# The first chunk's triangular inverses: squarings on TensorE against a 16x16 solve on VectorE, in a two-stage kernel on one Trainium2 core

## The chip, the cores and the metric

The kernel runs on one core of one Trainium2 chip. Its time is the device time of one execution in microseconds (us), of which smaller is better. The span is the part of an execution that the profiler's records cover.

## The reference

Two stages follow each other. The first is a recurrence over 768 steps for each of 4 x 8 heads, with a state of 40 x 40:

```python
for t in range(S):                      # S = 768; r, k, v, w, a, b are (4, 8, 768, 40), float32
    y[:, :, t] = np.einsum('bhd,bhde->bhe', rt, state)
    Sa = np.einsum('bhde,bhe->bhd', state, at)
    state_decay = state * wt[:, :, None, :] - np.einsum('bhd,bhe->bhde', Sa, bt)
    state = state_decay + np.einsum('bhd,bhe->bhde', vt, kt)
```

Its output, as x of 3072 x 320 (heads side by side), goes through a feed-forward block with an exact GELU:

```python
h = x @ w_in                            # w_in is 320 x 2048, passed as 64-bit floats
g = 0.5 * h * (1.0 + erf(h * inv_sqrt2))
out = (g @ w_out).astype(np.float32)    # w_out is 2048 x 320, passed as 64-bit floats
```

## The kernel before

**Chunks.** The 768 steps are cut into 12 chunks of C = 64. Within a chunk the recurrence is written as products: masked 64 x 64 matrices between the columns of a, b, k, r and v, which are scaled by running products of w. Each of the 32 heads needs the inverse of one unit triangular 64 x 64 matrix, whose strict part is N. Two blocks of 32 x 32 on its diagonal are inverted, and a product of three joins them. NBL = 16 heads lie side by side in the free dimension, and two batches one above the other in the 128 partitions.

**Steps.** Every piece of work is a small function marked `@step`; a suffix names the chunk. For chunk c the steps that matter here are these.

- `lg`, `cu`, `ec`, `wT`, `ew`: logarithm of w, running sums by matmuls (L717, L708), their exponentials.
- `sb`, `sk`: b and k scaled by these decays (L796, L801). `sk.0` runs on GpSimd before, `sk.1` and `sk.2` on VectorE.
- `ta`, `tb`, `tk`, `tr`, `tv`: turned on TensorE in chunks 0 to 2 (L763), copied out by `sa`, `sn`, `kc`, `rc`, `vc`.
- `nm`, `am`, `vm`: the 64 x 64 products (L188); `nk`, `ak`, `vk` mask them on VectorE (L876).
- `nd`, `nx`, `iz`, `ic`, `wx`: for chunks 1 to 11 the 32 x 32 inverses by column elimination on GpSimd (L957, L959, 62 operations for a chunk). `nx` brings N into the tile `Nb`, `iz` sets the tile `W` to the identity, `wx` takes the result to `Tt`.
- `tc_`, `jm`, `jc`, `wb`, `km`, `kt0`, `kt1`, `wa`: the joining product.
- `av`, `xm`, `xc0`, `xc1`, `sm`, `sc`, `pk`, `pb`, `oa`, `od`, `om`: the chunk's result and the next state. For chunk 0 `xp` and `xe` (L1244) bring the result into `xt`, for others `ox` by DMAs.
- `mh` (eight per chunk, L1308), `ge`: x @ w_in and the GELU; chunk 0 then has four `pm` (L1429), and the others seven products `m1` to `m7` (L1347, with sums `s1` to `s4`, `e1` to `e6` on VectorE and ScalarE) for g @ w_out.
- `Lf`, `Lf5`, `Ls`: the weights as 64-bit words, in 18 units; `ce`, `cs`, `cm`, `cv` (or `cl`, `cn`, `cg`, `cx`, `cy`) turn each unit into 32-bit floats. Units 0 to 9 are w_in. Unit 9 lies in the memory of `xt` until `cv.9` has read it, so `xe` comes behind `cv.9`.
- `warm_first`, `warm`: matmuls whose results nobody reads.

**Chunk 0.** Its 32 x 32 inverses are made otherwise: as a product of (I + N^(2^k)). `qt`, `qi`, `qs` start it; `qm.0` to `qm.4` multiply on TensorE, `qz` turns on VectorE, `qb` and `qs` split into two halves on VectorE and ScalarE, `qc` copies on ScalarE, `qa` adds on VectorE; `ql` and `qx` place the result, and `jm.0`, `jc.0`, `km.0` join with forms of their own.

**Order.** One text, `order`, names every step once, and the program is issued in just this order. Each engine works through its own instructions in it, and waits only where data or a buffer asks for it. PSUM is held as four tiles `bank0` to `bank3`, taken in turn by `take` and given back by `drop`; all DMAs of the stretch discussed here are issued from SyncE, in the order's sequence.

Of the kernel before, what the change touches and what calls it, by code (L numbers as in the profile page):

```python
# [1467 lines left out]
```

## Time and profile before

| | |
|---|---|
| median of 3 runs | 632.1 us (631.37 to 632.44) |
| profiled execution | 632.67 us, span 630.9 us |
| mean granted TensorE clock | 0.995 |
| busy: TensorE matmuls, weight loads | 619.7 us (98%), 521.8 us (83%) |
| busy: VectorE, ScalarE, GpSimd | 454.4 (72%), 345.4 (55%), 369.6 us (59%) |
| DMA | 63.97 MB, mean 101 GB/s |

In the profile PE is TensorE's matmuls, PEld its weight loads, DVE VectorE, ACT ScalarE, POOL GpSimd, SP SyncE. A line number is that of the kernel before; L188 is the helper `mm`, so matmuls of many steps carry it and are told apart by their tiles. Matmuls overlap, so the time from the first start to the last end of a group says more than its mean. A matmul of 32-bit floats in the source is two instructions in the trace. The granted clock is in shares of full speed. The profiled execution lies 1.8 us over its own span and 0.6 us over the median.

### The profile page before, as it was taken

To read this page: it belongs to the slowest core of one execution; us is meant where nothing else is said; L and a number is where in the kernel's file an instruction comes from. 1 tells how busy PE (TensorE), PEld (TensorE's weight loads), DVE (VectorE), ACT (ScalarE), POOL (GpSimd) and SP (SyncE) were. 2 spreads that over 40 slices of the span, in tenths; PEclk is the share of its full clock that TensorE was granted. 3 is DMA by queue.
4 is the path that set the end of the run, shared out by engine and by line. 5 is a ranking of instruction groups with operands and counts; after the bars stand their busy time and mean duration, and the time that the engine had idled before them with its cause. 6 is when DMAs were issued, how large, how long until landed. Compare 5 with 4: busy or idle time off the path is not lost.

```text
span 630.9 us, 31485 instructions
## 1 busy us (share of the span) xinstructions
PE 619.7 (98%) x14196; PEld 521.8 (83%) x14196; DVE 454.4 (72%) x558; ACT 345.4 (55%) x475; POOL 369.6 (59%) x797
## 2 busy tenths in 40 slices
PE   8989999999999999999999999999999999999997
PEld 5777787777987987987987988987988978978977
DVE  1788998875979978996886785875867955744313
ACT  4866897685454637636654647445557435243020
POOL 6278565738814875868848818838813886830000
PEclk9998999999999999999999999999999999999999
DMA  9997887722555766665575554444663454110100
GB/s 153 166 155 166 188 181 175 132 62 47 117 109 86 146 116 119 128 124 102 98 133 101 108 108 87 83 77 96 123 132 51 85 87 86 34 25 4 43 3 21
DMA packets 246550, 63.97 MB, mean 101 GB/s; under 512 B 228216, under 2 KB 243328, under 8 KB 246416
## 3 DMA queue, kind: packets, MB, share of 16 engines
q1 hardware_dynamic: 245976, 61.68, 52.0%
q8 instruction: 111, 1.82, 1.2%
q10 hardware_dynamic: 440, 0.29, 0.2%
q14 instruction: 23, 0.19, 0.1%
HBM read 54.39 MB, written 3.93 MB: 92 GB/s over the span
## 4 chain that ended last, share of the span: by engine, by line
PE 95%; ACT 1%; DVE 1%; SPq 1%; issue 1%; DMA 0%; DVEq 0%; ACTq 0%
PE bank L1308 33%; PE bank L188 30%; PE bank L1347 27%; PE bank L1429 3%; PE bank L763 2%; SPq L479 0%; SPq L1226 0%; DMA xt<-xt 0%; ACT st L1016 0%; DVE os L1298 0%; ACT L727 0%; ACT N L918 0%; DVE N L876 0%; ACT kT L727 0%; ACT gt L1313 0%
## 5 line engine op out<-in xcount | busy, mean ns | idle before, releaser
L1308 PE MATMUL bank<-xt,w_in_sb 64*64 64x256 f32 x3840 | 220.5, 377 | 1.1 <-DMA xt<-xt 1.1
L957 POOL TENSOR_TENSOR tmp<-W,Nb 128x126 f32<-128x126 f32 (+22 forms) x341 | 156.9, 460 | 77.3 <-DVE Nb L923 51.7
L1308 PEld LDWEIGHTS bank<-xt,w_in_sb 64*64 64x64 f32 x3840 | 147.1, 133 | 52.1 <-issue 1.8
L959 POOL TENSOR_TENSOR W<-W,tmp 128x126 f32<-128x126 f32 (+22 forms) x341 | 163.7, 480 | 26.7
L1347 PE MATMUL bank<-w_out_sb,gt 128*128 128x160 f32 x704 | 102.0, 302 | 0.2 <-ACT gt L1313 0.2
L1347 PEld LDWEIGHTS bank<-w_out_sb,gt 128*128 128x128 f32 x704 | 96.6, 190 | 3.5 <-issue 1.3
L1313 ACT ACTIVATE gt<-bank 128x1024 f32<-128x1024 f32 x48 | 49.1, 1024 | 73.1 <-PE bank L1308 71.9
L1152 DVE TENSOR_TENSOR SM<-bank,upper 128x832 f32<-128x832 f32 (+1 forms) x24 | 22.9, 989 | 19.5 <-PE bank L188 19.4
L1262 ACT COPY conv<-st 32x128 f32<-32x128 f32 (+2 forms) x55 | 28.0, 510 | 14.5 <-DVE st L1256 13.7
L1298 DVE TENSOR_TENSOR os<-os,bank 128x160 f32<-128x160 f32 x44 | 14.0, 319 | 28.5 <-PE bank L1347 19.1
L1347 PE MATMUL bank<-extra,conv 128*128 128x160 f32 x208 | 30.0, 299 | 0.0
L1313 ACT ACT_TABLE_LOAD x23 | 29.5, 1283 | 0.4
L1298 DVE TENSOR_TENSOR conv<-gt 128x1024 f32<-128x1024 f32 x11 | 14.0, 1272 | 21.0 <-ACT gt L1313 21.0
L1347 PEld LDWEIGHTS bank<-extra,conv 128*128 128x128 f32 x208 | 28.9, 190 | 0.0
L1204 DVE TENSOR_TENSOR st<-bank,st 128x832 f32<-128x832 f32 (+1 forms) x22 | 21.2, 986 | 8.8 <-PE bank L188 8.8
L1347 PE MATMUL bank<-extra,gt 128*128 128x160 f32 x176 | 26.4, 303 | 0.2 <-DVE os L1298 0.2
L734 DVE TENSOR_TENSOR_SCAN kT<-spare,kT 128x256 f32<-128x256 f32 x36 | 26.1, 782 | 0.6 <-ACT kT L727 0.6
L1347 PEld LDWEIGHTS bank<-extra,gt 128*128 128x128 f32 x176 | 24.3, 190 | 1.5 <-issue 0.9
L942 POOL MEMSET W<- 128x512 f32 x11 | 5.8, 525 | 32.9 <-DVE Tt L928 32.9
L801 POOL TENSOR_TENSOR bk_rows<-bk_rows,part 128x640 f32<-128x640 f32 x9 | 14.5, 1614 | 14.1 <-DMA bk_rows<-in_k_dram 14.1
L699 ACT ACT_TABLE_LOAD x11 | 14.1, 1283 | 13.8 <-DMA w_tile<-in_w_dram 13.7
L754 ACT ACT_TABLE_LOAD x11 | 14.1, 1283 | 13.1 <-PE bank L188 12.7
(227 smaller groups left out, 1156.1 us busy)
## 6 DMA issues: line engine op xcount, KB each, us to landing
bk_rows<-in_b_dram SPq DMA_DIRECT2D x24, 160.0 KB
bk_rows<-in_k_dram SPq DMA_DIRECT2D x24, 160.0 KB
out_dram<-os SPq DMA_DIRECT2D x46, 80.0 KB
VR<-in_v_dram SPq DMA_DIRECT2D x22, 160.0 KB
w_tile<-in_w_dram SPq DMA_DIRECT2D x36, 80.0 KB
v_pairs<-in_w_dram SPq DMA_DIRECT2D x18, 144.0 KB
a_pairs<-in_a_dram SPq DMA_DIRECT2D x18, 144.0 KB
a_pairs<-in_b_dram SPq DMA_DIRECT2D x18, 144.0 KB
```

Of the source, the lines that this page charges most:

```text
L188: nc.tensor.matmul(o, lhsT, rhs, start=first, stop=True, skip_group_check=True)
L734: nc.vector.tensor_tensor_scan(logs[:, at:at + n], onward, logs[:, at:at + n], 0.0, ALU.mult, ALU.add)
L957: nc.gpsimd.tensor_tensor(t, W[:, BL // 2 - rows:, rest:rest + 1].to_broadcast([P, rows, rest]), Nb[:, rest:rest + 1, :rest].to_broadcast( ...
L959: nc.gpsimd.tensor_tensor(own, own, t, ALU.add)
L1152: nc.vector.tensor_tensor(SM[:, g, :, :, cols], pair_of(f"S{c}_", g).rearrange("p x i c -> p i x c")[:, :, :, cols], kept, ALU.mult)
L1204: nc.vector.tensor_tensor(to, pair_of(f"QY{c}_", g)[:, :, :, cols], to, ALU.add)
L1262: nc.scalar.copy(apart.rearrange("p e i g d -> p (e i g) d")[to_rows, :, to_col:to_col + n], st.rearrange("p e i g c -> p (e i g) c")[rows ...
L1298: nc.vector.tensor_tensor(to, one_, other, how)
L1308: nc.tensor.matmul(ph[half(x ^ y), x, s], w_in_sb[half(x), kt, at:at + HP], xt[half(x), kt], start=kt == 0, stop=kt == NK - 1, skip_group_ ...
L1313: nc.scalar.activation(gt[:, 4 * q:4 * q + 4].rearrange("p (x s) t -> p x s t", x=2), bank(f"ph{c}_{q}").rearrange("p x (s t) -> p x s t", ...
L1347: nc.tensor.matmul(po[:, n, :DM // 2], l_[:, f], r_[:, f], start=f == 0, stop=f == NF // 2 - 1)
L1429: nc.tensor.matmul(po[:, g, :DM], gt[:, f, g * P:(g + 1) * P], w_out_sb[:, f], start=f == 0, stop=f == NF - 1)
```

## The change

Chunk 0's 32 x 32 blocks are no longer inverted by squarings. Each is cut into two blocks of 16 x 16; `dx` and `dh` bring all of them into `N_16`, `dz` sets `W_16` to the identity, and `de` solves them by column elimination on VectorE, 15 columns of two operations each. `dw` and `dt` bring the result to `Tt`, `tc_.0` turns it; `dm`, `dj`, `dk.0`, `dl`, `dk.1`, `da` join the 16 x 16 blocks to 32 x 32 in both orientations by products on TensorE: 64 products of 32 x 32 by 32 x 16 in `dm`, 32 in `dk.0`, 64 in `dk.1`. From there chunk 0 uses `jm`, `jc`, `wb`, `km`, `wa` as the other chunks do. `sk.0` runs on VectorE. The tile `of_half` and the steps `diagonal_set` and `of_half_set` go, `parity` gets a third row. `N_16`, `W_16` and the turned blocks lie in the tile `Nb`, and `dj` writes into the tile `W`. The order text is another one throughout, for all twelve chunks; `one_set` stands late in it. The branches of `iz`, `ic` and `L_of` for chunks from 12 on, which no chunk took, are gone.

```diff
-        eng.tensor_tensor(T_, stacked, diagonal.unsqueeze(1).to_broadcast([P, NBL, BL]), ALU.add)
-    def qm(k):
-        take(f"sq{k}", (2, 3, 3, 3, 1)[k])
...
+    QL = BL // 2
+    turned_16 = Nb_tile[:, :QL * BL]
+    N_16 = Nb_tile[:, QL * BL:QL * BL + QL * QL].rearrange("p (t s) -> p t s", s=QL)
+    W_16 = Nb_tile[:, QL * BL + QL * QL:].rearrange("p (t s) -> p t s", s=QL)
+    J_16 = W_tile.rearrange("p (n t) -> p n t", t=BL)
+    T_of_0 = flat(Tt)[:, :, BL:]
...
+    def dx():
+        nc.vector.transpose(turned_16.rearrange("p (t n z) -> p t n z", n=NBL, z=2),
+                            halves(flat(N_of(0))[:, :, :BL]))
+    def dh():
+        both = turned_16.rearrange("p (t z s) -> p t z s", z=2, s=QL)
+        nc.vector.scalar_tensor_tensor(N_16, both[:, :, 0], parity[:, 0, 0:1], both[:, :, 1], ALU.mult, ALU.add)
+    def de(j0, j1, q):
+        for u in range(QL - 1 - j0, QL - 1 - j1, -1):
+            n = QL - u
+            t = tmp_tile[:, :n * u].rearrange("p (s t) -> p s t", s=n)
+            own = W_16[:, u:, :u]
+            eng.tensor_tensor(t, W_16[:, u:, u:u + 1].to_broadcast([P, n, u]),
+                              N_16[:, u:u + 1, :u].to_broadcast([P, n, u]), ALU.mult)
+            eng.tensor_tensor(own, own, t, ALU.add)
+    def dw(z, q):
+        to, keep = turned_16.rearrange("p (t z s) -> p t z s", z=2, s=QL)[:, :, z], parity[:, z, 0:1]
+        if q == "a":
+            nc.scalar.mul(to, W_16, keep)
+        else:
+            nc.vector.tensor_scalar(to, W_16, keep, None, ALU.mult)
+    def dt():
+        nc.vector.transpose(halves(T_of_0), turned_16.rearrange("p (t n z) -> p t n z", n=NBL, z=2))
+    def dm():
+                mm(J[rows, n, :QL], N[rows, n, own], L_tile[rows, n, :QL])
+    def dj():
+        nc.scalar.mul(J_16[:, :, :QL], J[:, :, :QL], parity[:, 2, 0:1])
+    def dk(z):
+                if z:
+                    mm(K[rows, n, :QL], J_16[rows, n], T_of_0[rows, n, QL:])
+                elif q % 2 == 0:
+                    mm(K[rows, n, :QL], T_of_0[rows, n], J_16[rows, n, :QL])
+    def dl(x):
+        nc.vector.tensor_tensor(own, K[lo[x], :, :QL], own, ALU.add)
+    def da():
+        nc.vector.tensor_tensor(own, K[:, :, :QL], own, ALU.add)
```

The order up to the first `mh`, where TensorE's steps stand in this sequence. Before:

```
warm_first warm.4.4 cu.0 wT.0 ta.0 tb.0 warm.4.2 nm.0 cu.1 warm.4.15 wT.1 qm.0 warm.4.20 tb.1 ta.1 qm.1 nm.1 cx.1 tk.0
qm.2 warm.4.0 am.0 qm.3 tr.0 tv.0 qm.4 vm.0 jm.0 warm.4.13 av.0 km.0 cu.2 sm.0 warm.4.18 pk.0 pb.0 tv.1 wT.2 tb.2 ta.2
xp.0 tk.1 nm.2 xp.1 tr.1 am.1 tk.2 warm.4.24 vm.1 mh.0.0
```

After:

```
warm.4.13 warm.4.20 warm.4.25 cu.0 wT.0 tb.0 ta.0 nm.0 cu.1 wT.1 tv.0 warm.4.18 warm.4.4 warm.4.15 warm_first ta.1 dm
tb.1 tr.0 dk.0 dk.1 warm.4.24 nm.1 tk.0 cx.1 jm.0 vm.0 am.0 cu.2 km.0 av.0 tv.1 sm.0 tk.1 ta.2 pk.0 pb.0 wT.2 xp.0 xp.1
tr.1 tb.2 vm.1 nm.2 warm.4.0 am.1 mh.0.2
```

VectorE's steps of the new order from `nk.0` to `xe.1`:

```
nk.0 dx dh de.0.5 de.5.10 de.10.15 dw.1 dt tc_.0 sb.1 cs.0 cs.1 cm.0 cv.0 cm.1 sa.1 dl.0 da dl.1 sk.0 cs.2 cm.2 nk.1 cv.2
nx.1 cy.1 vk.0 ak.0 sk.1 cs.3 cm.3 cv.3 xc1.0 kt1.0 cs.4 cm.4 cv.4 sc.0.0 sc.0.1 cs.5 cm.5 cv.5 od.0.0 om.0.0 om.0.1 cs.6
cm.6 od.0.1 cs.7 cm.7 cv.7 sb.2 sa.2 cs.9 cm.9 cv.9 vk.1 xe.1
```

More of the change, by code (lines that the diff above doesn't have):

```diff
@@ L363, in diagonal_set @@
     @step
-    def diagonal_set():
-        for q in range(P // BL):
-            rows = slice(q * BL, (q + 1) * BL)
-            nc.gpsimd.tensor_copy(diagonal[rows], ident[rows, rows])
-    @step
     def sums_mask():
@@ new lines, in dw @@
+    @step
+    def dw(z, q):
[4 more added lines that the diff above has]
+            nc.vector.tensor_scalar(to, W_16, keep, None, ALU.mult)
+    @step
+    def dt():
+        nc.vector.transpose(halves(T_of_0), turned_16.rearrange("p (t n z) -> p t n z", n=NBL, z=2))
+    @step
+    def dm():
+        N = flat(N_of(0))
+        J = take("D0")[:, 0].rearrange("p (n t) -> p n t", n=NBL)
+        for n in range(NBL):
+            for q, rows in enumerate(quads):
+                own = slice(q % 2 * BL, (q % 2 + 1) * BL)
+                mm(J[rows, n, :QL], N[rows, n, own], L_tile[rows, n, :QL])
@@ L1434, in pc @@
         drop(f"po{c}")
-    for token in order(NCH, NS):
+    for token in order():
         perform(steps, token)
```

329 lines of the change are left out of this document (132 added, 197 removed).

## The prediction

> **What bounds the kernel.** I read the page first: busy times and the chain that ended last.
>
> ```profile
> PE 619.7 (98%) x14196; PEld 521.8 (83%) x14196; DVE 454.4 (72%) x558; ACT 345.4 (55%) x475; POOL 369.6 (59%) x797
> ...
> PE 95%; ACT 1%; DVE 1%; SPq 1%; issue 1%; DMA 0%; DVEq 0%; ACTq 0%
> ```
>
> TensorE is nearly always busy and makes 95% of the chain. But a share over the whole span hides that the start is of another kind. So I cut the span by windows, at the start of the squarings (17.9), of chunk 0's `sm` (55.3), of the first `mh` (78.9) and of the first `pm` (101.3). The columns after the length are PE, PEld, DVE, ACT, POOL, granted clock, DMA share, GB/s.
>
> ```profile
> 0.00:17.90 17.90, 15.22 (x132) 9.10 (x132) 3.82 (x6) 9.31 (x11) 10.29 (x57) 1.00 0.97 159
> 17.90:55.30 37.40, 34.27 (x818) 27.52 (x817) 30.07 (x48) 28.55 (x41) 22.98 (x50) 0.91 0.93 153
> 55.30:78.90 23.60, 23.56 (x510) 19.09 (x512) 22.20 (x38) 18.40 (x25) 14.92 (x33) 1.00 0.84 190
> 78.90:101.30 22.40, 22.40 (x644) 18.35 (x632) 19.96 (x30) 20.85 (x31) 9.92 (x20) 1.00 0.83 176
> 101.30:631.00 529.70, 524.23 (x12119) 447.75 (x12112) 378.35 (x439) 268.27 (x372) 311.45 (x638) 1.00 0.47 89
> ```
>
> From 78.9 on TensorE is idle for 5.5 of 552.1 us. So the end moves with the start of the first `mh`, plus whatever work lies behind it. Before that, TensorE's busy share includes fillers (`warm`), squarings and slow matmuls, and VectorE is close behind. The start is therefore the place where this change is won or lost. In finer windows, one dip shows in it:
>
> ```profile
> 42.00:44.00 2.00, 1.96 (x80) 1.71 (x76) 1.93 (x5) 1.82 (x4) 1.76 (x4) 1.00 1.46 170
> 44.00:46.00 2.00, 0.08 (x5) 0.08 (x7) 1.90 (x3) 0.64 (x1) 1.76 (x4) 0.71 0.66 73
> 46.00:48.00 2.00, 2.00 (x66) 1.88 (x68) 0.66 (x2) 1.86 (x2) 1.69 (x5) 0.50 0.93 160
> 48.00:50.00 2.00, 2.00 (x28) 1.04 (x24) 1.97 (x4) 1.32 (x4) 1.76 (x4) 0.50 0.66 93
> ```
>
> After a gap of 1.9 us at 44 the granted clock is 0.50 until 50, so "busy" there is half work.
>
> The timeline gives the landmarks: `nm.0` begins at 14.06, the first squaring step on VectorE at 17.90, the last copy into `xt` (`xe.1`) ends at 75.45, the first `mh` starts at 78.92.
>
> ```profile
> 14.06 1.16 PE L188 MATMUL bank<-aT,nT 40*64 40x64 f32 x64 [0.24 <-ACT nT L813]
> 17.90 0.71 DVE L979 STREAM_TRANSPOSE st<-N 128x512 f32<-128x512 f32 x1 [1.31 <-ACT N L918]
> 74.77 0.68 DVE L1244 COPY xt<-bank 128x512 f32<-128x512 f32 x1
> 78.92 4.53 PE L1308 MATMUL bank<-xt,w_in_sb 64*64 64x256 f32 x80
> ```
>
> **Part 1, TensorE's queue up to the first mh.** From 14.06 to 78.92 it took 64.86 us.
>
> ```profile
> 31.26 2.08 PE L188 MATMUL bank<-turned,st 64*64 64x64 f32 x64
> 46.76 1.92 PE L188 MATMUL bank<-st,N 32*32 32x32 f32 x64
> 52.69 1.20 PE L188 MATMUL bank<-turned 32*32 32x32 f32 x64
> 99.53 0.75 PE L188 MATMUL bank<-turned,spare 32*32 32x32 f32 x64
> 22.67 1.12 PE L188 MATMUL bank<-cum_m,ident 128*128 128x512 f32 x2
> 48.61 2.08 PE L188 MATMUL bank<-cum_m,ident 128*128 128x512 f32 x2
> 76.05 1.09 PE L763 MATMUL bank<-ident,extra 128*128 128x128 f32 x8
> ```
>
> Out go five squarings (5 x 2.08 = 10.4). `jm.0` and `km.0` fall from 1.92 and 1.20 to the 0.75 of the other chunks' form (1.6). The fillers 13 and 20 move ahead of `nm.0` (2.08 and 1.12), and `tk.2` moves behind the first `mh` (1.09). That is 16.3. In come `dm` and `dk`: 160 products, 320 instructions. The row of 64 instructions in 0.75 us gives 11.7 ns each, so 3.75 us; at a squaring's 2.08 for 64 it would be 10.4, the upper end. I take 3.75, since these are 32 x 32 tiles as in that row, with fewer columns. `warm.4.4` comes in for 1.12 and `warm_first`, six instructions of a filler's size, for 3 x 1.12 = 3.4. Together 8.2. The queue is 8.1 shorter, and with all its old waits still in it, it reaches the first `mh` at 14.06 + 56.8 = 70.8.
>
> [...]
>
> In front of `nm.0` nothing is gained: it waits for the copy of b's transposes (the row's wait on ACT nT), whose loads, w, b and a, are still the first three in SyncE's queue. Fewer fillers there only mean more idle time, up to 14.06.
>
> **Part 2, VectorE's queue from the first solve step to xe.1.** This is the other queue that the first `mh` waits for.
>
> ```profile
> 17.90:75.45 57.55, 49.35 (x80) 0.94 0.89 162
> ```
>
> Here the column after the length is VectorE alone: 49.35 busy, 8.2 idle. The next rows are those that go (L979 to L1031), and those that price what comes.
>
> ```profile
> L1009 DVE STREAM_TRANSPOSE st<-bank 128x512 f32<-128x512 f32 x4 | 2.9, 713 | 2.4 <-PE bank L188 2.4
> L1018 DVE TENSOR_SCALAR st<-st,of_half 128x512 f32<-128x512 f32 x5 | 2.8, 568 | 0.1
> L1026 DVE TENSOR_TENSOR turned<-turned,bank 128x512 f32<-128x512 f32 x4 | 2.7, 680 | 0.7 <-PE bank L188 0.4 <-ACT turned L1004 0.3
> L979 DVE STREAM_TRANSPOSE st<-N 128x512 f32<-128x512 f32 x1 | 0.7, 714 | 1.3 <-ACT N L918 1.3
> L984 DVE TENSOR_TENSOR turned<-N,rT 128x512 f32<-128x512 f32 x1 | 0.7, 650 | 0.0
> L1031 DVE STREAM_TRANSPOSE st<-turned 128x512 f32<-128x512 f32 x1 | 0.7, 711 | 0.1
> L1298 DVE TENSOR_TENSOR os<-os,bank 128x160 f32<-128x160 f32 x44 | 14.0, 319 | 28.5 <-PE bank L1347 19.1 <-ACT os L1392 7.8 <-DVE os L1298 0.5
> L422 DVE STREAM_TRANSPOSE parity<-Js 128x64 f32<-128x64 f32 x1 | 0.2, 240 | 0.0
> L801 DVE TENSOR_TENSOR extra<-bk_rows,part 128x640 f32<-128x640 f32 x1 | 1.4, 1402 | 0.0
> L801 DVE TENSOR_TENSOR extra<-bk_rows,os 128x640 f32<-128x640 f32 x1 | 0.8, 783 | 0.0
> 27.52 1.55 POOL L801 TENSOR_TENSOR extra<-bk_rows,part 128x640 f32<-128x640 f32 x1 [15.68 <-DMA bk_rows<-in_k_dram]
> 37.39 1.21 DVE L876 TENSOR_TENSOR nT<-bank,upper 128x1024 f32<-128x1024 f32 x1
> ```
>
> The squarings' rows sum to 10.5. `parity_set` (0.24) moves ahead, `nk.2` (1.21) and `sk.2` (1.40) move behind: 13.4 out. In come three transposes of 128x512 (`dx`, `dt`, `tc_.0`, 2.1), and `dh`, `dw`, two `dl` and `da`, of 256 elements or so. A line through the sums of 160 elements (319 ns) and 512 (650) costs these at 0.41 each, 2.05. `de` is 30 operations of n times u elements, 15 to 64, on average 45: 680 over the 15 columns. The same line gives 0.21, and I take 0.23 with the gap behind a dependent one: 6.9. Its ends are 0.15 and 0.32, 4.5 and 9.6 in all, since no row has so small a sum. `sk.0` costs 0.78 to 1.40 here (rows of `sk.1` and `sk.2`) in place of 1.55 on GpSimd; I take 0.78, since GpSimd's long solve, beside which `sk.2` ran, hasn't begun. `vk.1` moves in (1.21). Sum 13.0, so 49.0 busy.
>
> The size of the idle time is the choice. Of the 8.2, L1009, L1026 and the wait of `kt1.0` for the slow `km.0` make nearly 5: waits of squarings for TensorE. They go. New waits come: for `dw.0` on ScalarE, for `dk`, for `pb.0`. I take 5.5. Then `xe.1` ends at 17.9 + 49.0 + 5.5 = 72.4. TensorE's 70.8 lies under it, but TensorE is at `sm.0` before VectorE has done `kt1.0`, which stands behind `cv.3`, and the half clock may come again there. For that I add 1.2 and put the first `mh` at 73.6, 5.3 earlier than 78.9.
>
> **Part 3, what lies beside these.** Behind the first `mh` the new order holds what the old held, with `tk.2` more (1.09; one filler stands for another). So the end comes 5.3 - 1.1 = 4.2 earlier. GpSimd starts chunk 1's solve later, since `nx.1` stands behind the first chunk's solve in VectorE's queue and shares its tile.
>
> ```profile
> 31.11 1.25 DVE L923 STREAM_TRANSPOSE Nb<-spare 128x1024 f32<-128x1024 f32 x1
> 32.50 0.24 POOL L957 TENSOR_TENSOR tmp<-W,Nb 128x31 f32<-128x31 f32 x1 [1.44 <-DVE Nb L923]
> 69.92 0.25 POOL L959 TENSOR_TENSOR W<-W,tmp 128x16 f32<-128x16 f32 x1
> 57.07 2.52 SPq L561 DMA_DIRECT2D xt<-in_moe_w_in_dram  x4
> ```
>
> It took 37.7 us. By the sum of VectorE's queue `nx.1` comes near 44, so `wx.1` near 82 and `tc_.1` near 87. `jm.1` stands some 16 us of TensorE's work behind the first `mh`, near 89: covered, by about 2 us. Without that cover it costs what it overruns, one for one. SyncE's queue issues the pieces of w_in's unit 9 (the row of xt, 57.07 to 59.59) behind 32 loads where it was 31, so they land later by about one load's issue, 1 to 3 us; `cv.9`, near 70, has that behind it. The loads of chunk 0 and w_in's first half stand earlier or no more than a few places later. ScalarE loses some 5 us of halves and copies; it bounds nothing.
>
> From 101 on TensorE binds in both orders, and I find the last products (`m1.11` to `m4.11`) in nearly the same sequence; I count no difference, up to 2 us either way.
>
> **Forecast.** The profiled execution's 632.67 less 4.2 is 628.5; on the median, 632.1 - 4.2 = 627.9. With VectorE's idle time from 3 to 8 us, it is 625.4 to 630.4.
>
> **Rivals.** *VectorE becomes the bound (slower).* The 30 small operations take 0.40 instead of 0.23, as in-place operations that wait each for the one before: 5.1 more. With the old 8.2 of idle time and the 1.2 above, the first `mh` starts at 17.9 + 49.0 + 5.1 + 8.2 + 1.2 = 81.4: 632.1 + 2.5 + 1.1 = 635.7. For it: VectorE is busy in 30.07 of 37.40 us already, and weight conversions queue behind the solve. Against: the 160-element row at 0.32 lies above every one of these. It decides from a first `mh` after 79.1 (1.3 us over the break-even of 77.8).
>
> *Given back in waits (no change).* VectorE idles 9 to 10 us, since the chain `km.0`, `kt1.0`, `sm.0`, `sc.0` passes through its queue twice; the first `mh` comes near 77.8, and the time stays near 632. For it: 7.3 of the 8.2 fell in the stretch of the old solve. Against: those were mostly waits for squarings.
>
> *TensorE bound throughout (faster still).* VectorE idles 2, TensorE keeps its clock and loses 2 of its waits; the first `mh` comes at 69, so 632.1 - 9.9 + 1.1 = 623.3. Against: `sm.0` waits for `kt1.0`.
>
> **Numbers.** A measurement can tell about 0.2%, 1.3 us. Forecast 0.50, faster still 0.10, no change 0.13, slower 0.27. So faster 0.60, same 0.13, slower 0.27. The range leaves out a tenth beyond the slower rival and a little below the fastest: 622.5 to 636.0; the forecast's own is 625.4 to 630.4.
>
> **What would show it.** Right: L1308 first starts at 71 to 76; the 30 operations of `de` at 0.2 to 0.25 each; 320 instructions of `dm` and `dk` in under 5 us; VectorE idle 4 to 7 from `dx` to `xe.1`; from there TensorE idle for not more than 7 us. Wrong: a `de` over 10 us, half clock for more than 5 us, TensorE waiting at `jm.1` for `tc_.1`, or a first `mh` that comes early and an end that doesn't, with idle time in the last 500 us.

## The result: 1.5% slower, with stretches in which TensorE waited for its own instructions

The changed kernel took 641.8 us (median of 4 runs, 638.87 to 643.78) against 632.3 us (631.37 to 632.78) for the kernel before: a ratio of 1.0149, interval 1.0107 to 1.0190. The forecast was 627.9, the range ended at 636.0. The direction and the range were wrong.

The profiled execution took 642.18 us, its span is 640.5. From the page of the changed kernel, busy times and the chain that ended last:

```profile
PE 618.7 (97%) x14196; PEld 523.7 (82%) x14196; DVE 457.9 (71%) x581; ACT 335.7 (52%) x464; POOL 375.9 (59%) x792
...
PE 83%; issue 4%; ACT 3%; POOL 3%; DMA 3%; DVE 2%; SPq 1%; ACTq 0%; POOLq 0%; DVEq 0%
```

TensorE did as many instructions as before and was busy for 1.0 us less, in a span 9.6 us longer. So the whole loss is time in which TensorE did nothing, and slow time counted as busy. "issue", time in which an engine waits for nothing that the profile shows, rose from 1% to 4% of the chain.

The windows at the changed kernel's own landmarks (first `nm.0`, `sm.0` at 61.53, first `mh` at 82.24, first `pm` at 114.91), with the first stretch cut where the clock changes:

```profile
14.21:29.98 15.77, 12.95 (x230) 8.96 (x232) 11.79 (x38) 8.92 (x12) 0.00 (x0) 1.00 1.18 167
29.98:47.05 17.07, 15.82 (x357) 12.50 (x346) 10.82 (x20) 8.89 (x14) 1.21 (x5) 0.50 0.95 143
47.05:61.53 14.48, 10.93 (x359) 8.85 (x357) 9.50 (x15) 8.64 (x13) 11.79 (x29) 0.88 0.90 172
61.53:82.24 20.71, 20.10 (x470) 16.30 (x469) 19.69 (x32) 14.80 (x22) 16.11 (x25) 1.00 0.68 163
82.24:640.50 558.26, 548.98 (x12762) 471.06 (x12752) 403.39 (x475) 287.14 (x399) 336.56 (x683) 1.00 0.48 91
```

For 17 us behind the solve the clock is at half, and VectorE is busy in 10.82 of 17.07. The first `mh` starts 3.3 us later than before (78.92), not 5.3 earlier. From there to the end it takes 558.3 us where it took 552.0: 6.3 more, of which `tk.2` accounts for the 1.1 forecast.

The timeline of TensorE shows the idle stretches. The bracket holds the idle time ahead of a row and what ended it:

```profile
29.32 1.59 PE L185 MATMUL bank<-turned,N 32*32 32x16 f32 x128 [2.82 <-DVE turned L946]
33.72 1.65 PE L746 MATMUL bank<-ident,r_pairs 128*128 128x128 f32 x7 [0.70 <-issue]
38.55 1.15 PE L185 MATMUL bank<-Tt,W 32*32 32x16 f32 x71 [0.56 <-issue]
56.09 0.18 PE L185 MATMUL bank<-T,Js 32*32 32x32 f32 x1 [3.55 <-issue]
134.98 4.57 PE L1403 MATMUL bank<-w_out_sb,gt 128*128 128x320 f32 x16 [0.73 <-issue]
249.30 0.21 PE L185 MATMUL bank<-T,Js 32*32 32x32 f32 x2 [1.34 <-issue]
428.38 0.87 PE L185 MATMUL bank<-aT,nT 40*64 40x64 f32 x44 [1.57 <-issue]
```

The first is the wait of `dm` for `tc_.0`. The others fall into the middle of steps (`km.0` stops for 3.55 us after 38 of its 64 matmuls), with no wait for data. Of such unexplained stretches of 0.25 us or more, the kernel before has two, 2.3 us in all:

```profile
45.93 0.91 PE L188 MATMUL bank<-rT,late 40*64 40x64 f32 x20 [1.92 <-issue]
110.51 0.57 PE L188 MATMUL bank<-SM,Tt 64*64 64x104 f32 x10 [0.38 <-issue]
```

The changed kernel has seven, 8.7 us; the seventh, of 0.26 us, is at 339.

**What they have in common.** The page's row of DMA queue 8, kind "instruction", gives packets and MB: first the kernel before (the changed one has the same row), then an experiment with 1024 more TensorE instructions, then one with 504 fewer.

```profile
q8 instruction: 111, 1.82, 1.2%
```

```profile
q8 instruction: 115, 1.88, 1.2%
```

```profile
q8 instruction: 109, 1.79, 1.2%
```

Four packets more for 1024, two fewer for 504, one for every 256; both kernels have 111, of 16.4 KB each (1.82 MB over 111). The changed kernel's trace has 28,492 records of TensorE, and 111 times 256 is 28,416. The first packet begins at 17.15 us in the changed kernel, the last at 625.24. So I read them as TensorE's program, which comes by DMA in blocks of 256 instructions while the kernel runs. I counted TensorE's records (matmuls, weight loads and its few others) ahead of each unexplained stretch of 0.25 us or more, in all 20 traces of this study: in 115 of 116 the count is 193 or 194 above a multiple of 256, and it is 193 in all nine of the two profiles above. That place is called a border below. In none of the 20 traces did TensorE pass a border sooner than 2.17 us after the record of that block's transfer began (2.40 in the kernel before, 2.30 in the changed one), and the nine stretches ended 1.25 to 1.61 us behind the end of that record. So I take an "issue" stretch here as TensorE waiting for its next block. The section on the kernel before has it that an engine waits only where data or a buffer asks for it; at these nine places TensorE stood still for 0.26 to 3.55 us, and by the profile neither did. The expectations call this the fetch theory. Their clock theory is that the half clock comes from the wait for `tc_.0`, and that the late start comes from the half clock.

### The profile page after: what moved, and what is told of

The parts are those of the page before. It is cut to its first block, busy times and chain, and to the rows that moved or that the text cites. A ratio compares the mean times of both kernels' runs of the same rounds, so it can differ in the third digit from the quotient of the medians.

```text
span 640.5 us, 31483 instructions
## 1 busy us (share of the span) xinstructions
PE 618.7 (97%) x14196; PEld 523.7 (82%) x14196; DVE 457.9 (71%) x581; ACT 335.7 (52%) x464; POOL 375.9 (59%) x792
## 3 DMA queue, kind: packets, MB, share of 16 engines
q8 instruction: 111, 1.82, 1.2%
## 4 chain that ended last, share of the span: by engine, by line
PE 83%; issue 4%; ACT 3%; POOL 3%; DMA 3%; DVE 2%; SPq 1%; ACTq 0%; POOLq 0%; DVEq 0%
PE bank L1282 28%; PE bank L1321 27%; PE bank L185 24%; PE bank L1403 3%; PE bank L746 1%; DMA w_tile<-in_w_dram 1%; POOL W L938 1%; POOL tmp L936 1%; DMA bk_rows<-in_moe_w_out_dram 1%; DMA gt<-in_moe_w_in_dram 1%; SPq L574 1%; POOL conv L655 1%; DVE Nb L983 1%; DVE tmp L981 1%; ACT gt L1287 0%
## 5 line engine op out<-in xcount | busy, mean ns | idle before, releaser
L936 POOL TENSOR_TENSOR tmp<-W,Nb 128x126 f32<-128x126 f32 (+22 forms) x341 | 162.4, 476 | 81.4 <-DVE Nb L906 55.9
L1282 PEld LDWEIGHTS bank<-xt,w_in_sb 64*64 64x64 f32 x3840 | 150.9, 134 | 50.4 <-issue 1.3
L938 POOL TENSOR_TENSOR W<-W,tmp 128x126 f32<-128x126 f32 (+22 forms) x341 | 167.1, 490 | 26.7
L1236 ACT COPY conv<-st 32x128 f32<-32x128 f32 (+2 forms) x55 | 28.0, 509 | 12.4 <-DVE st L1230 11.6
L1126 DVE TENSOR_TENSOR SM<-bank,upper 128x832 f32<-128x832 f32 (+1 forms) x24 | 22.9, 988 | 16.3 <-PE bank L185 16.2
L1272 DVE TENSOR_TENSOR conv<-gt 128x1024 f32<-128x1024 f32 x11 | 13.7, 1249 | 23.5 <-ACT gt L1287 23.5
L1356 ACT COPY os<-bank 128x160 f32<-128x160 f32 x11 | 3.2, 292 | 36.7 <-PE bank L1321 36.6
L1321 PE MATMUL bank<-extra,SM 128*128 128x160 f32 x144 | 21.3, 301 | 0.0
```

What stands on the lines that cost most here:

```text
L936: eng.tensor_tensor(t, W[:, BL // 2 - rows:, rest:rest + 1].to_broadcast([P, rows, rest]), Nb[:, rest:rest + 1, :rest].to_broadcast([P, ro ...
L938: eng.tensor_tensor(own, own, t, ALU.add)
L1126: nc.vector.tensor_tensor(SM[:, g, :, :, cols], pair_of(f"S{c}_", g).rearrange("p x i c -> p i x c")[:, :, :, cols], kept, ALU.mult)
L1236: nc.scalar.copy(apart.rearrange("p e i g d -> p (e i g) d")[to_rows, :, to_col:to_col + n], st.rearrange("p e i g c -> p (e i g) c")[rows ...
L1272: nc.vector.tensor_tensor(to, one_, other, how)
L1282: nc.tensor.matmul(ph[half(x ^ y), x, s], w_in_sb[half(x), kt, at:at + HP], xt[half(x), kt], start=kt == 0, stop=kt == NK - 1, skip_group_ ...
```

## The experiments

Ratios are to the kernel before in the same session. First `mh` (before 78.92, changed 82.24) and idle stretches come from each profile, one execution.

**1. The same kernel again, and fillers in place of the wait for `tc_.0`.** `again` is unaltered. `fill`:

```diff
-dm
+warm.4.30 warm.4.31 warm.3.32 dm
```

> The changed kernel once more, nothing altered. Fetch theory (TensorE's idle stretches that nothing in the profile explains are waits for its own instructions, which come in blocks of 256): the same number of matmuls and weight loads, 193 more than a multiple of 256, has started ahead of every such stretch over 0.25 us; their lengths vary by up to 2 us between executions, which would make the scatter of 0.8%. Clock theory: half clock from about 30 to 47 again, behind the wait for tc_.0. Rival (they are disturbances from outside): stretches at other places, no common remainder. Time 639 to 644 by all.

> The changed kernel with three more fillers (2.9 us of matmuls that nobody reads) just ahead of dm, where TensorE waited 2.8 us for tc_.0. Clock theory: no gap at 26.5 to 29.3, granted clock 1.00 and not 0.50 from 30 to 47 (at most one stretch of 3.4 us at half), the products of dk, nm.1 and am.0 take half as long, first mh at 77 to 79 in place of 82.2, time 637 to 639. Rival (the chain of the solve through VectorE and ScalarE sets the start whatever TensorE's clock is): clock full, but first mh still at 81 to 83 and time 641 to 643. Fetch theory: with 12 more instructions ahead the unexplained stretches fall into other steps, again at 193 above a multiple of 256.

`again`: 641.3 us, 1.015 (1.0105 to 1.0195). Its four unexplained stretches, at 32.92 (1.08 us), 52.35 (3.40), 246.99 (0.99) and 424.97 (1.53), come behind the same counts as four of the seven above, so they belong to the program; three small ones are missing. Half clock for 17.1 us from 30.1. `fill`: 643.0 us, 1.018 (1.0132 to 1.0228), first `mh` at 82.72. The wait is down to 0.47 us and the half clock shorter (6.8 us twice), but these rows of its timeline came in their place:

```profile
35.88 0.83 PE L186 MATMUL bank<-Tt,W 32*32 32x16 f32 x77 [1.98 <-issue]
51.51 0.22 PE L186 MATMUL bank<-Tt,Js 32*32 32x32 f32 x2 [1.96 <-issue]
59.95 0.37 PE L186 MATMUL bank<-ident,VR 128*64 128x128 f32 x1 [4.51 <-issue]
```

What the clock theory forecast (fill the gap, gain 3 to 5 us) didn't come. But `fill` also moves every border behind it by 12 instructions, so it doesn't test the gap alone.

**2. Which half of the order costs.** One kernel has the new order up to the first `mh` and then what is left in the old sequence; the other the old order with its squarings, then the new sequence.

```diff
-order = new
+order = new[:first mh] + [t for t in old if not in new[:first mh]]    # new_head_old_tail
+order = old[:first mh] + [t for t in new if not in old[:first mh]]    # old_head_new_tail
```

> The order of the changed kernel up to the first mh, from there the steps that are left in the sequence of the kernel before. Theory that the late order costs (about 5 us of idle TensorE behind the first mh come from the new sequence there): first mh at 82 to 84, at most 2 us idle from there to the last products, time 635 to 636.5. Rival (the late sequence is as good as the old one, and the delay of the start is handed on): 640 to 643. Fetch theory: the late idle time is a matter of where the borders of 256 instructions fall, so some 0 to 4 us of unexplained stretches, in other steps than before: 634 to 639.

> The order and the squarings of the kernel before up to the first mh, from there the steps that are left in the new sequence. Theory that the late order costs: first mh at 79 as before, then 4 to 6 us of idle TensorE, time 636 to 638. Rival (all of the loss comes out of the start): 631 to 633. Fetch theory: some 0 to 4 us of unexplained stretches behind the first mh, each at 193 above a multiple of 256, time 632 to 636.

`new_head_old_tail`: 643.4 us, 1.0183 (1.0141 to 1.0225). It says little: the steps left over at the seam put the first `mh` at 88.4 and added a wait of 2.06 us for VectorE. `old_head_new_tail`: 635.7 us, 1.0060 (1.0035 to 1.0085), 6.3 us idle behind 80 us, 3.4 us of half clock at 425. So the late sequence costs about 0.6% without the solve. That the start costs the other 0.9% is a difference and was not measured alone.

**3. Moving the borders alone.** Tiny products ahead of `nm.0`, read by nobody, shift every later border by 4 instructions each; no other step moves.

```diff
-nm.0
+pad.8.0 nm.0      # 32 instructions; pad.40.0: 160 instructions
+    def pad(n, i):
+        pt = take(f"pad{i}")
+        for x in range(n):
+            mm(pt[:BL, 0, :BL // 2], ident[:BL, :BL], cum_m[:BL, :BL // 2])
+        drop(f"pad{i}")
```

> The kernel before with 40 tiny products (160 instructions of TensorE, 0.4 to 0.9 us, read by nobody) ahead of nm.0, which move every border of 256 instructions by 160. Fetch theory: the borders fall into denser runs, where the 304 instructions up to a border took under 3.8 us: near 99, 195, 243, 368, 435 and 487 unexplained stretches of 0.6 to 1.8 us, 5 to 9 us of idle time in all behind the first mh where there were 1.7, perhaps a stretch at half clock behind the longest; time 637 to 643. Rival (the unexplained stretches belong to the order or to the steps in which they were seen, not to the count of instructions): slower by the tiny products alone, 632.5 to 633.5.

> The kernel before with 8 tiny products (32 instructions) ahead of nm.0. Fetch theory: its borders stay outside the dense runs but for one near 245 us (0.7 us): 0 to 0.4% above the kernel before. Rival (any movement of the borders costs this tuned order 1% and more): 1 to 2% above.

> The changed kernel with 8 tiny products (32 instructions) ahead of nm.0, where TensorE waits 1.5 us anyway. Fetch theory: the borders at 134, 249, 339 and 428 move out of their dense runs, at most 1 us of unexplained stretches is left behind the first mh where there were 3.9, and the half clock behind 428 goes; the start stays much as it is. Time 636.5 to 639.5. Rival (the stretches belong to the steps): unchanged at 641 to 643.

> The changed kernel with 40 tiny products (160 instructions) ahead of nm.0. Fetch theory: denser borders both in the start (near 35 and 46) and behind it (near 241, 276, 369, 376, 418): 8 to 14 us more idle time and half clock than in the changed kernel, time 2.5 to 4% above the kernel before, near the kernel before with the same products (3.1% above). Rival (only the changed order is prone to stretches, wherever its borders fall): 1.3 to 2%.

> The old start and squarings with the new sequence behind the first mh (635.7 us), with 8 tiny products ahead of nm.0. Fetch theory: the stretches near 131, 245 and 422 and the half clock at 425 go, some 5 us less: 631 to 633.5, so that the new late sequence is as good as the old one where the borders fall well. Rival (the late sequence itself costs 3 to 4 us): 635 to 637.

| instructions added | order before | changed order |
|---|---|---|
| 0 | 1 | 1.0149 (1.0107 to 1.0190) |
| 32 | 0.9981 (0.9956 to 1.0005) | 1.0102 (1.0043 to 1.0161) |
| 160 | 1.0307 (1.0272 to 1.0343) | 1.0295 (1.0257 to 1.0333) |

The kernel before loses 3.1% by 160 useless instructions. They took longer than I had put (80 matmuls in 2.70 us in `after_pad160`), but `nm.0` started only 2.1 us later; 11 unexplained stretches of 9.7 us, all at borders, and 3.4 us of half clock four times make up most of the rest. With 160 added, the two orders cost the same. With 32 the changed kernel's profile has its first `mh` at 73.68, against the 73.6 forecast and 82.24 without them: 3.4 us of half clock instead of 17. All 160 products of `dm` and `dk` are in it. But that is the fastest of four executions, which lie between 637.5 and 645.8, and their ratio's interval overlaps that of the unpadded kernel. The stretch near 428 stayed (1.99 us at 417.5, 6.8 us of half clock behind it), another came (1.34 at 494.8), and my list of which would go was wrong. `old_head_new_tail_pad32` (1.0053, 1.0033 to 1.0073) didn't gain at all: the stretches near 131 and 422 stayed. Counting instructions finds where a stretch can be, but not whether it comes: of the 111 borders in the changed kernel's profile seven have one of 0.25 us or more.

**4. The transfers beside it.** `light` leaves out the ten loads of the second half of w_in (GpSimd zeroes their memory, the second half of the hidden layer is computed from zeros).

```diff
-Lf.0.1.1 Lf.0.0.1 Lf.1.1.1 Lf.2.1.1 Lf.1.0.1 Lf.2.0.1 Lf5.1.0 Lf5.1.1 Lf.3.0.1 Lf.3.1.1
+zero_set.0 zero_set.1 zero_set.2 zero_set.3 zero_set.4      # earlier, behind dz
```

> The changed kernel without the ten loads of the second half of w_in (GpSimd sets their memory to zero early, so the second half of the hidden layer is computed from zeros). Tells what the transfers of 40 to 60 us do to the fetches. Fetch theory with crowded DMA: the fetch whose record began 3.9 us behind the border at 49.35 begins within 2 us, the stretch of 3.5 us in km.0 is under 1.5, first mh at 75 to 79, time 635 to 638. Rival (the fetch is late for a cause of its own): the stretch in km.0 stays at 3 us or more, first mh at 80 to 83.

639.1 us, 1.0065 (1.0039 to 1.0091), first `mh` at 79.29 in a profile of the fastest of ten executions (636.7). The record of the block in `km.0` began 2.0 us behind the previous border, where it had been 3.9 in the changed kernel, and the stretch there fell from 3.55 to 1.16 us. The stretch at 34 grew, from 0.70 to 1.96. So with fewer transfers beside it this block came earlier, as far as one execution of each shows; the transfers aren't the only cause, since in `old_head_new_tail_pad32` a record began 5.9 us behind the previous border at 122, where the DMA share was 0.53. The half clock (13.7 us) stayed.

**5. Splices that should have won.** `spliced` is the changed order with `pad.8.0` up to `mh.3.5`, then the old sequence; `spliced_off` has `pad.33.1` at the seam as well. The expectations put the seam near 320 us; the products of `pad.33.1` came to stand at 245 to 248.

```diff
+order = new[:mh.3.5], pad.8.0 ahead of nm.0, then the rest of old      # spliced
+... pad.33.1 at the seam                                               # spliced_off
+... pad.5.0 for pad.8.0; warm.4.30 warm.4.31 warm.3.32 ahead of dm     # spliced_fill
+... Lr.0 behind LV.0; tr.0 rc.0 vm.0 ahead of dm, vk.0 behind it       # spliced_vm
```

> The changed kernel with 8 tiny products ahead of nm.0, in the new order up to mh.3.5 (near 320 us) and from there the steps that are left in the sequence of the kernel before, whose borders then lie 27 instructions from where they lie in the kernel before. Fetch theory: first mh at 73 to 75 with no stretch over 1.5 us ahead of it but the wait for tc_.0, behind 330 us at most 1 us of unexplained stretches (where the changed kernel with the 8 products had 4 and a half clock of 6.8 us), time 0.3 to 0.9% below that of the kernel before. Rival (the new solve and its order are the slower ones, and the early first mh was luck of one execution): 0.3 to 1% above.

> The same spliced order with 33 tiny products (132 instructions, 0.8 to 1.6 us) at the splice near 320 us, which move the borders behind it alone. Fetch theory: unexplained stretches of 3 to 6 us behind 320 us (near 368, 435, 487 and 562 by the old order's dense runs), 4 to 8 us slower than without them. Rival (only the products' own time): 1 to 1.6 us slower.

> The spliced order with three fillers (2.9 us) ahead of dm in place of the wait for tc_.0, and 5 tiny products instead of 8 ahead of nm.0, so that all borders behind dm stay where they were. Clock theory: the executions at 644 to 647 go, all lie at 635 to 640, median 636 to 638, and the profile has no long half clock in the start. Rival (the two groups have another cause): both groups stay, or all executions move together.

> The spliced order with Lr.0, tr.0, rc.0 and vm.0 (144 instructions of TensorE) moved ahead of dm, into the time of the solve on VectorE, and vk.0 behind dm. Fetch theory for the start (too many dense products stand behind the solve, and blocks of 256 take 4 to 7 us each there): the wait for tc_.0 falls to under 1 us, half a block less behind it, first mh 2 to 4 us earlier than the 77.5 of the spliced kernel's profile, time 632 to 636. Rival (VectorE's and ScalarE's chain sets the first mh): first mh 76 to 79, time 636 to 640.

`spliced`: 1.0084 (1.0048 to 1.0119); its profile, of an execution of 637.4 us, has the first `mh` at 77.52 and nothing unexplained of 0.4 us or more behind it, yet its executions lie in two groups (635.7 to 639.6 and 644.0 to 646.6). `spliced_off`: 1.0206 (1.0164 to 1.0249), 7.6 us more than `spliced`, as the fetch theory had it, for products of 2.3 us. `spliced_fill`: 1.0120 (1.0088 to 1.0152), one execution at 636.2 and five at 640.6 to 643.0; its profile has a stretch of 1.69 us at a border at 35.1 and 10.2 us of half clock behind it. So here half clock came without the wait for `tc_.0`. `spliced_vm`: 1.0161 (1.0140 to 1.0182), first `mh` at 84.65, stretches of 3.44 and 3.69 us at borders: the 144 instructions moved ahead of `dm` only changed which steps were cut. I found no version that beats the kernel before; `before_pad32` can't be told from it.

**6. The supply by itself.** Multiples of 256 instructions leave every later border on its old instruction. `before_pad256` has 256 ahead of `nm.0`; `before_pad1024` has 1024 late in the run (they came to stand at 234 us, not near 290), as products in four tiles side by side.

```diff
+side.16.0 nm.0           # before_pad256
+side.64.1 mh.3.6         # before_pad1024
+    def side(n, i):
...
+                rows = slice(q * BL, (q + 1) * BL)
+                mm(pt[rows, 0, :BL // 2], ident[rows, rows], cum_m[rows, :BL // 2])
```

> The kernel before with 64 tiny products (256 instructions, in four tiles side by side, some 1.6 us) ahead of nm.0: more added work than in the runs with 8 and 40 products, but every border behind it falls on the same instruction as in the kernel before. Fetch theory: the late part is as in the kernel before (at most 2 us of idle time behind the first mh); one wait of 1 to 2 us for a block near nm.0; in all 0.1 to 0.6% above the kernel before. Rival (any addition in the tuned start shifts the work and costs, as with 160 instructions 3.1%): 2% and more.

> The kernel before with 256 tiny products (1024 instructions, four blocks) near 290 us, where TensorE sets the time; no border behind it moves. It measures the supply by itself. Rival (TensorE issues small matmuls at the 12.4 ns of dm, nothing else limits it): 512 matmuls take 6.4 us, time 6 to 7 us more (1.0%). Fetch theory: a block of 256 isn't followed by the next in under 3.6 to 4.2 us, however fast it is used up: 13 to 17 us more (2.0 to 2.7%), TensorE idle in three or four stretches of 2 to 2.7 us, each at 193 or 194 above a multiple of 256.

`before_pad256`: 1.0065 (1.0043 to 1.0086), 4 us where 160 instructions cost 19. Behind the first `mh` its idle stretches are 1.9 us, as in the kernel before. What it lost, it lost at the start: a wait of 3.39 us for a block in `nm.0`, 6.8 us of half clock from 17.2 on, and a first `mh` at 84.34. `before_pad1024`: 652.4 us, 1.0300 (1.0279 to 1.0322), 18.7 us more. TensorE's timeline:

```profile
233.80 1.23 PE L189 MATMUL bank<-cum_m,ident 32*32 32x16 f32 x125
237.43 1.69 PE L189 MATMUL bank<-cum_m,ident 32*32 32x16 f32 x128 [2.40 <-issue]
241.70 1.90 PE L189 MATMUL bank<-cum_m,ident 32*32 32x16 f32 x128 [2.59 <-issue]
245.98 1.90 PE L189 MATMUL bank<-cum_m,ident 32*32 32x16 f32 x128 [2.38 <-issue]
249.71 0.29 PE L189 MATMUL bank<-cum_m,ident 32*32 32x16 f32 x3 [1.83 <-issue]
```

Three runs of exactly 128 matmuls (256 instructions with their loads), each used up in 1.7 to 1.9 us, one every 4.3 us. The 512 matmuls took 16.2 us, where the rate of the first row gives about 5. This is the disputed cost alone, far from the start; the DMA share was 0.89 from 234.39 to 237.80 and 0.49 in the 17.07 us behind that; in the start of the kernel before (17.90 to 55.30) it was 0.93. The clock was at half for these 17.07 us, too:

```profile
237.80:254.87 17.07, 10.28 (x411) 7.94 (x404) 1.65 (x2) 0.00 (x0) 0.00 (x0) 0.50 0.49 87
```

**7. Fewer instructions in the start, every wait left in place.** `few1` replaces the 64 products of `dm` by one wide product of the same tiles, `few2` those of `dk.1` too; chunk 0's inverses are then computed from other values.

```diff
-                mm(J[rows, n, :QL], N[rows, n, own], L_tile[rows, n, :QL])      # 64 of them
+        mm(J, N[:, :2].rearrange("p n t -> p (n t)"), L_tile)
-                    mm(K[rows, n, :QL], J_16[rows, n], T_of_0[rows, n, QL:])    # 64 of them, few2 only
+            mm(K, W_tile[:, :P], T_of_0)
```

> The changed kernel with the 64 products of dm (256 instructions) replaced by one wide product of the same tiles (4 instructions, 1.0 to 1.1 us where dm took 1.6), so chunk 0's inverses are computed from other values. Borders behind it move by 4. Fetch theory: one block less between the solve and the first mh, first mh 3 to 6 us earlier than 82 (76 to 79), time 636 to 639, 0.5 to 0.9% less than the changed kernel. Theory of the wait and the half clock: the wait for tc_.0 and the half clock of 17 us stay, first mh 81 to 82, time within 1 us of the changed kernel.

> As before, and the 64 products of dk.1 (256 instructions) by one wide product too: two blocks less. Fetch theory: first mh at 72 to 77, no stretch over 2 us between 30 and 60 but waits for data, time 632 to 636. Theory of the wait and the half clock: first mh 80 to 82, time within 2 us of the changed kernel. Theory of the chain through VectorE: first mh not under 79 in either.

`few1`: 639.0 us, 1.0098 (1.0068 to 1.0128); the profiled execution was the longest of its four, with the first `mh` at 81.44 and three stretches at borders (1.46, 2.01, 2.63 us) between 37 and 59. `few2`: 632.0 us, 0.9991 (0.9973 to 1.0008), 1.6% less than the changed kernel. Its windows behind the solve and behind the first `mh`, and the timeline rows of `dm`, of `xe.1` on VectorE and of the first `mh`:

```profile
29.70:46.80 17.10, 16.25 (x474) 11.60 (x478) 16.63 (x28) 14.83 (x22) 5.32 (x17) 1.00 0.83 143
...
73.00:630.00 557.00, 548.47 (x12759) 471.62 (x12748) 402.13 (x475) 287.41 (x399) 337.69 (x685) 1.00 0.50 93
```

```profile
29.68 1.12 PE L185 MATMUL bank<-turned,N 128*128 128x512 f32 x2 [2.82 <-DVE turned L946]
...
72.96 1.29 PE L1280 MATMUL bank<-xt,w_in_sb 64*64 64x256 f32 x17
```

```profile
71.14 0.67 DVE L1216 COPY xt<-bank 128x512 f32<-128x512 f32 x1
```

The wait for `tc_.0` is still there, but the clock stays at 1.00, VectorE is busy in 16.63 of 17.10, and the first `mh` starts 9.3 us earlier than in the changed kernel, for some 0.9 us less work on TensorE (twice 1.59 to 1.12). Its ten executions lie between 631.4 and 634.6. So with wide products in place of 128 small ones the start is as early as forecast; `few1` shows that replacing half of them isn't enough. What counts of the small products, `few2` doesn't separate: the wide ones are 504 instructions fewer, which also moves the later borders by 8, and their tile is 128*128 in the row above, where that of `dm` was 32*32.

**What the traces show of the half clock.** In the changed kernel's profile the granted clock is 0.50 from 29.98 to 47.05, from 57.28 to 60.70 and from 429.34 to 432.75, and 1.00 around these. The times between its changes are 17.07, 10.24, 3.41, 368.64 and 3.41 us, all multiples of 3.41 us; the one stretch at half in the kernel before, 6.83 us from 44.85, is twice that. Each comes behind idle time: in the 3.41 us ahead of it TensorE was busy for 0.66, 1.19 and 1.85 us in the changed kernel, for 2.52 in the kernel before. But that alone doesn't tell where half clock came: from 50.46 to 53.87 the changed kernel's TensorE was busy for 2.09 us, and full clock followed. Nor did a busy TensorE end it: in the five times 3.41 us from 29.98 on it was busy for 3.04, 3.09, 2.85, 3.41 and 3.42. In eight profiles the wait for `tc_.0` (2.8 us) has half clock at its end or just behind it, of 17.07 us in `new_head_old_tail`, `again` and the changed kernel, of 3.41 us in `after_pad32`, `spliced`, `after_pad160`, `few1` and `spliced_off`. In `few2`'s profile the same wait has none. What makes these differences no run shows. But `few2`'s ten executions have mean granted clocks of 0.995 to 1.000, against 0.979 to 0.989 in the changed kernel's four: at most 6.3 us at half, against 14 to 27 (estimates, twice the missing share of the span). So the gain of `few2` isn't luck of one execution.

## Why the prediction was wrong, point by point

**VectorE's work was right.** The 30 operations of `de`, forecast at 0.23 with gaps, 6.9 in all:

```profile
L983 DVE TENSOR_TENSOR Nb<-Nb,tmp 128x15 f32<-128x15 f32 (+7 forms) x15 | 3.1, 207 | 0.5
L981 DVE TENSOR_TENSOR tmp<-Nb 128x15 f32<-128x15 f32 (+7 forms) x15 | 3.1, 206 | 0.6
```

They ran from 19.64 to 26.83, 7.2 us. `dx` and `dt` took 1.06 each instead of 0.71. From `dx` to `xe.1` VectorE was busy for 49.5 us; the sum said 49.0.

**The step that failed first is the price of `dm` and `dk`: 3.75 us for 320 instructions at 11.7 ns, at full clock.** They took 6.0. `dm`'s 128 matmuls did take 1.59 us, 12.4 ns each; the 192 of `dk`, at half clock and cut by a stretch, 4.4 us (35.30 to 39.70). The price was that of execution alone. The 320 matmuls have 320 weight loads, 640 instructions, 2.5 blocks, and the sum put nothing for fetching them. An estimate from experiment 6, where dense blocks came every 4.3 us, is 10.7 us for these; from the start of `dm` to the end of `dk.1` it was 10.4, with 16 matmuls of `tb.1` and `tr.0` in between. The squarings were as many matmuls, but among other work: in the kernel before the borders from 22.31 to 45.93 came 5.1 to 6.8 us apart, and the one stretch of 1.92 us, at 44, came behind the squarings. The rows of 128 in experiment 6 ran at 13 to 15 ns a matmul and then stopped.

**The step that failed next, and cost most, is VectorE's idle time, 5.5 us.** It was 13.3 (62.84 us from `dx` at 17.96 to the end of `xe.1` at 80.80, less 49.5). Waits for TensorE make 10.7 of it, by the view of waits from 18 to 82; the longest are these:

```profile
DVE SM L1105 <- PE bank L185: 3.0, 1, 3.0
DVE turned L1030 <- PE bank L185: 2.7, 1, 2.7
DVE Tt L1037 <- PE bank L185: 2.1, 1, 2.1
```

These are `xc1.0` behind the stretch in `km.0`, and `dl.0` and `da` behind `dk.0` and `dk.1` at half clock. I had sums for both queues, but took TensorE's as free to run, with its instructions at hand, and at full clock but for 1.2 us at `sm.0`. In `few2` the sums came near: VectorE was idle for 3.7 us from `dx` to `xe.1`, which ended at 71.8 (forecast 72.4), the first `mh` started at 72.96 (73.6). With the first `mh` at 82.24 instead of 73.6, 8.6 us of the miss lie in the start, and 5.1 behind it.

**"I count no difference behind 101" failed as well.** Stretches over 0.2 us behind 80 us rose from 1.7 to 5.5 us, and 3.4 us of half clock came behind the one at 428. `old_head_new_tail` puts a price of 0.6% on the new sequence, at its own place of the borders. `few2` has such stretches too: from its first `mh` to the end it takes 557.1 us, where the kernel before takes 552.0, 1.1 of it for `tk.2` and 3.2 for longer idle stretches. So it only ties with the kernel before, in spite of its early start.

**The rivals.** "VectorE becomes the bound" had a first `mh` of 81.4 and 635.7 us, close to the start measured, for the wrong reason: its operations cost 0.21, not 0.40. "Given back in waits" had the right kind of loss and half its size. None had the late part. Of the signs of being wrong, half clock for more than 5 us came true; idle time in the last 500 us came, too, but without the early first `mh` that it was named with. The cover of `jm.1` held (TensorE didn't wait there for `tc_.1`).

**What stays open.** How much of the late start is the supply of blocks and how much the half clock: `few2` takes away most of both, and no run takes away the one and leaves the other. And which borders become stretches: the blocks' records begin from 4.7 us ahead of the previous border to 5.9 behind it. A steering of the borders past all dense runs wasn't found.

## What to carry to other kernels

Price small matmuls twice, by their time and by their number. Here, in a long dense run (`before_pad1024`), a block of 256 TensorE instructions (128 matmuls with their loads) followed the last after 4.3 us, 17 ns an instruction (an estimate, 4.3 us over 256), with TensorE idle for 1.83 to 2.59 us ahead of each; the 256 instructions of `dm` took 1.59 us, 6.2 ns each. A single block can follow sooner: 1.5 us in `fill` at 31, where its record had begun 4.7 us ahead of the previous border. Then look at the granted clock behind each wait: 17.07 us at 0.50 behind the 2.82 us in the changed kernel, none behind the same wait in `few2`. An unexplained "issue" stretch in the middle of a step is worth a count of the instructions ahead of it; if several share a remainder of 256, as 115 of 116 did here, an edit anywhere ahead shifts them all, and a comparison of two orders measures that shift, too (here up to 3%), so compare them at more than one place of the borders.

## What the runs showed of the hardware that I had not expected

- DMA queue 8 moved one packet of 16.4 KB for every 256 instructions of TensorE (111 packets, 115 with 1024 instructions more, 109 with 504 fewer). TensorE passed no border sooner than 2.17 us after the block's record began (2.30 in the changed kernel), and 1.2 to 1.9 us after its end where it had waited (1.25 to 1.61 in the changed kernel and the one before). In the start the record began up to 4.9 us behind the previous border (3.85 in the changed kernel), once elsewhere 5.9.
- The half clock came in stretches of 3.41 us or multiples: 3.41, 6.83, 17.07 us. It followed idle stretches of 1.57 us (428 us, changed kernel) and 1.92 us (44 us, before), while the 2.82 us ahead of `dm` in `few2` had none behind it.
- Matmuls of 32 x 16 in four tiles side by side ran at 10 to 15 ns each (125 in 1.23 us, 128 in 1.90, `before_pad1024`), on one tile at 34 (80 in 2.70 us, `after_pad160`).
- A 128 x 512 transpose with a split order on one side took 1.06 us (`dx`), without it 0.71 (`tc_.0`).
